# Padding tiles that move the weights against the columns in SBUF: an fp32r attention-plus-GLU kernel

## The chip, the cores and the metric

The kernel runs on one core of a Trainium2 chip. The metric is the device time of one execution in microseconds. Before the change the median of three runs is 695.43 us (695.39 to 695.55). The page of the profile is of one further execution, which took 695.5 us.

The engines are called as the profile calls them: PE (TensorE matmuls), PEld (its weight loads, which overlap the matmuls), DVE (VectorE), ACT (ScalarE), POOL (GpSimd) and SP (SyncE, which here issues most DMAs). SBUF is the on-chip memory that PE reads its two operands from.

## The reference

Two branches work on the same normalised input, and both are added to the input:

```python
xn = layernorm(x)                                   # x: 2048 tokens x 448
return x + A(xn, wq, wk, wv, wo, beta) + B(xn, w_gate, w_up, w_down)

# A: 16 heads of 28, in 4 segments of 512 tokens
q, k, v = xn @ wq, xn @ wk, xn @ wv
for s in range(4):
    p = softmax(q_s @ k_s.T * 28 ** -0.5 + causal_mask)
    num, den = phi(q_s) @ M, phi(q_s) @ z + 1e-6    # phi(t) = t + 1 if t > 0 else exp(t)
    o_s = g * num / den + (1 - g) * (p @ v_s)       # g = sigmoid(beta)
    M, z = M + phi(k_s).T @ v_s, z + sum(phi(k_s))
A = concat(o) @ wo

# B: hidden width 1792
B = (sigmoid(xn @ w_gate) * (xn @ w_up)) @ w_down
```

## The kernel before

The 2048 tokens are cut into 4 blocks of 512, and the 448 features into chunks of 128 partitions. Large products are made in fp32r on PE. Each operand is split into a high part (the value as fp32r rounds it) and a low part (the rest), and three partial products are added in PSUM: high by high, high by low, low by high. For a contraction of 448 this makes 11 matmuls to one PSUM tile (the list `TERMS`).

A matmul has two operands in SBUF: the *weights* (128 columns of one tile, brought into the array by a weight load ahead of it) and the *columns* that are then moved past them. In `T.matmul(out, weights, columns)` they are the second and the third argument. Five groups of fp32r matmuls matter here:

| line | PSUM tile | what | weights | columns | columns moved | matmuls |
|---|---|---|---|---|---|---|
| L241 | `pgu` | gate and up projections | `wgu` | `xs` | 512 | 1232 |
| L347 | `pp` | keys and queries | `wqk` | `xs` | 512 | 308 |
| L166 | `pd` | down projection | `hh` | `wdn` | 448 | 672 |
| L327 | `pv` | values | `xs` | `wv` | 448 | 176 |
| L763 | `po` | output projection | `xs` | `wo` | 448 | 176 |

A sixth one, L604 (`st`, 256 matmuls), makes the attention scores: weights and columns are both slices of one tile `qk2`, on 84 partitions, with 512, 384, 256 or 128 columns.

The order of the work on PE is written out by hand. A front phase (to about 155 us) makes the values, keys and queries. Then the generator `gated()` makes the GLU branch in groups of 11 `pgu` matmuls, with `pd` groups of 6 (in two halves of 3) between them, while `attention()` is stepped between these pieces and puts in the scores (`st`) and the products with the values (`pa`, L679). At the end `project()` makes the output projection, with the last `pd` groups between its first tiles. ACT and DVE split the weights and bring the results out of PSUM, POOL masks the scores, SP issues the loads.

Where a tile lies in SBUF follows from the order in which the pools are opened and from the sizes of their tiles. First comes the pool `keep` (`ident`, `xs`, `acc`, and the small `gate` and `gate_n`), then `mid` (the 8 KB tiles `wgu`, `wo`, the 4 KB tiles `hh`, and staging), then `late` (`wv`, later `wdn`, by the helper `late_pair`), then `front` (`wqk` and more, in the front phase) or `att` (`qk2` and more, later) behind it. All slices that these matmuls take are multiples of 256 bytes away from the start of their tile: 512 columns of fp32 are 2048 bytes, 128 are 512, and 448 are 1792, which is 7 times 256. So the address modulo 256 of an operand is that of its tile, and the difference between the two operands of a line is one number:

| line | columns, address mod 256 | weights, address mod 256 | columns minus weights, mod 256 |
|---|---|---|---|
| L241 `pgu` | `xs` 128 | `wgu` 192 | 192 |
| L347 `pp` | `xs` 128 | `wqk` 192 | 192 |
| L166 `pd` | `wdn` 192 | `hh` 192 | 0 |
| L327 `pv` | `wv` 192 | `xs` 128 | 64 |
| L763 `po` | `wo` 192 | `xs` 128 | 64 |
| L604 `st` | `qk2` 192 | `qk2` 192 | 0 |

In what follows "distance" is the number in the last column.

Of the kernel before, what the change touches and what calls it, by code (L numbers as in the profile page):

```python
# [9 lines left out]
F32 = mybir.dt.float32  # L10
F32R = mybir.dt.float32r
# [5 lines left out]
P = 128  # L17
# [44 lines left out]
def kernel(  # L62
# [13 lines left out]
    keep = ctx.enter_context(tc.tile_pool(name="keep", bufs=1))  # L76
# [7 lines left out]
    def split(hi, lo, src):  # L84
        A.activation(hi, src, AF.Copy)
        V.tensor_sub(lo, src, hi.bitcast(F32))
# [32 lines left out]
    gate = keep.tile([P, NG], F32, name="gate")  # L119
    gate_n = keep.tile([P, NG], F32, name="gate_n")  # L120

    def weigh(pool, num, g, add):

        r = pool.tile([P, 16], F32, name="rc", bufs=2)
        n3 = num.rearrange("p (m c) -> p m c", c=32)
        if add:
            V.tensor_scalar_add(r, n3[:, :, DH], add)
            V.reciprocal(r, r)
        else:
            V.reciprocal(r, n3[:, :, DH])  # L130
        V.scalar_tensor_tensor(n3[:, :, :DH], n3[:, :, :DH], g, r.unsqueeze(2).to_broadcast([P, 16, DH]),
                               op0=ALU.mult, op1=ALU.mult)
# [8 lines left out]
    def eight_k(dtype, name):  # L141
        return mid.tile([P, 8, 256], dtype, name=name, tag="8k")
# [7 lines left out]


    late = ctx.enter_context(tc.tile_pool(name="late", bufs=4, reuse_waits="tile"))

    def late_pair(name):
        return late.tile([P, 2, D], F32R, name=name, tag="late")

    rest, begin, wo = [], [], {}

    def gated():
# [33 lines left out]
            split(wdn[f][:, 0, :], wdn[f][:, 1, :], raw_down[f])  # L193

        def ready_out(h):
            wo[h] = eight_k(F32R, "wo").rearrange("p c n -> p (c n)")
            split(wo[h][:, :2 * D], wo[h][:, 2 * D:4 * D], raw_up[NF + h][:, :2 * D])

        begin.extend([lambda: ready_down(0), lambda: (ready_down(1), load_down(2)), lambda: ready_down(2)])
# [10 lines left out]
        for f0 in range(0, NF, FG):  # L210
# [7 lines left out]
            if f0 + FG < NF:  # L218
                ahead[1, 2] = lambda: ready_up(f0 + 2)
                if f0 > 0:  # L220
                    ahead[2, 1] = lambda: ready_down(f0 + 2)
                ahead[2, 3] = lambda: load_down(f0 + 3)
                ahead[2, 2] = lambda: load_up(f0 + 4)
                ahead[3, 2] = lambda: ready_up(f0 + 3)
                ahead[3, 3] = lambda: ready_down(f0 + 3)
                if f0 > 0:
                    ahead[0, 2] = lambda: (load_up(f0 + 3), load_down(f0 + 2))
            else:

                ahead[0, 2] = lambda: load_up(f0 + 3)  # L230
                ahead[1, 2] = lambda: ready_out(0)
                ahead[3, 2] = lambda: ready_out(1)
# [35 lines left out]

    with tc.tile_pool(name="front", bufs=2) as sb, tc.manual_schedule(engines=FRONT):
        heads = sb.tile([P, P], F32, name="heads", bufs=1)  # L270
        stage = eight_k(F32, "stage").rearrange("p (c a) n -> p c (a n)", c=4)
        vst = eight_k(F32, "vst").rearrange("p (t a) (h c) -> p t (a h) c", t=NT, c=32)
        wv = [late_pair("wv") for _ in range(4)]
# [115 lines left out]
        def recall(b, i, phi):  # L389
            ts = sb.tile([P, L], F32, name="ts", bufs=1)  # L390
            tb = sb.tile([P, L], F32, name="tb", bufs=2)
            n2 = bank("n2", ("m", "pd")[i % 2])
            T.matmul(n2, mst[b % 2][i], phi, start=True, stop=True)  # L393
            V.transpose(ts, n2)
            weigh(sb, ts, gate[:, i:i + 1], MEM_EPS)
            V.transpose(tb, ts)
            nc.gpsimd.dma_start(od[b][P * i:P * (i + 1)], tb)
# [98 lines left out]
        for b in range(NB):  # L496
# [24 lines left out]
            for k, c in enumerate((3, 4, 5, 6, 0, 1, 2) if last else range(7)):  # L521
# [34 lines left out]
                n = k - 1 if b == 0 else k + 1  # L556
# [16 lines left out]
    sb = ctx.enter_context(tc.tile_pool(name="att", bufs=1, reuse_waits="tile"))  # L573
# [88 lines left out]
    class Unit:  # L662
# [10 lines left out]
        def finish(self):  # L673

            s, i = self.s, self.i
            pa = bank("pa", "m")
            for kb in range(NT):
                for j in range(HG):
                    T.matmul(pa[32 * j:32 * j + 32, kb * P:], self.vv[:, kb, 32 * j:32 * j + 32],  # L679
                             self.pairs[j // 2].block(j % 2, kb), start=kb == 0, stop=kb == NT - 1)  # L680
            on, oc = (self.pairs[1].w[:, n * L:(n + 1) * L] for n in range(2))
            V.transpose(on, pa)
            yield
            weigh(sb, on, gate_n[:, i:i + 1], 0.0)
            V.transpose(oc, on)
            nc.gpsimd.dma_start(od[s][P * i:P * (i + 1)], oc, accum_op=ALU.add if s > 0 else ALU.bypass)
            yield
# [138 lines left out]
```

## Time and profile before

| what | value |
|---|---|
| median of the runs | 695.43 us |
| the profiled execution | 695.5 us |
| its span, first to last instruction | 693.8 us |
| PE busy | 688.1 us of the span |
| DVE busy | 570.4 us |
| ACT busy | 344.0 us |
| POOL busy | 147.7 us |
| granted TensorE clock | 1.00 |

The profile gives a matmul a start and a length. Matmuls are pipelined, so the length of one reaches over the start of the next one. What a matmul costs in a stream is therefore the time from its start to the start of the next; it is called its *step* here, and is read from two rows of the timeline: the difference of their starts, divided by the matmuls in the first row. The timeline merges equal instructions that follow each other, and gives the start of the first.

### The profile page before, as it was taken

The numbers are of one execution on the slowest core, as the hardware profiler recorded it, in microseconds if no ns is written. First come the engines' busy times: TensorE is split into PE (matmuls) and PEld (weight loads), VectorE is DVE, ScalarE is ACT, GpSimd is POOL, SyncE is SP. The second block draws the span as 40 slices with busy tenths as digits, with TensorE's granted clock in tenths as the row PEclk, the third lists the DMA queues.
The fourth block names the chain that finished last, engine by engine and source line by source line (L and its number), as shares of the span: only waits on it lengthen the run. The fifth ranks groups of instructions, "written<-read, shape, count | busy, mean of one in ns | idle before, by whom it ended". The sixth has DMA issues, their size and how long they took to land.

```text
span 693.8 us, 10446 instructions
## 1 busy us (share of the span) xinstructions
PE 688.1 (99%) x3594; PEld 565.7 (82%) x3594; DVE 570.4 (82%) x994; ACT 344.0 (50%) x563; POOL 147.7 (21%) x349
## 2 busy tenths in 40 slices
PE   8999999999999999999999999999999999999997
PEld 7898878778878787787878878787787878878897
DVE  6765785767889898988898889998889889889863
ACT  5836555343555456544555446455543555446320
POOL 3400020101223122221222223222232322222000
PEclk9999999999999999999999999999999999999999
DMA  7446566696242323233233342324342332333342
GB/s 265 180 147 236 196 220 228 255 326 169 70 99 73 92 86 85 69 118 106 56 71 93 74 127 56 98 56 115 81 113 57 95 71 68 86 87 88 96 149 106
DMA packets 45796, 84.37 MB, mean 122 GB/s; under 512 B 6320, under 2 KB 20400, under 8 KB 45232
## 3 DMA queue, kind: packets, MB, share of 16 engines
q1 hardware_dynamic: 42736, 76.37, 35.9%
q0 software_dynamic: 3008, 7.34, 5.2%
q8 instruction: 28, 0.46, 0.3%
q14 instruction: 24, 0.20, 0.1%
HBM read 51.05 MB, written 32.64 MB: 121 GB/s over the span
## 4 chain that ended last, share of the span: by engine, by line
PE 97%; DMA 1%; DVE 1%; SPq 0%; ACT 0%; issue 0%
PE pgu L241 42%; PE pd L166 20%; PE pp L347 10%; PE st L604 6%; PE pa L679 5%; PE po L763 5%; PE pv L327 4%; PE pmm L375 2%; PE n L393 1%; DMA acc<-in_x 1%; PE pt L95 1%; PE pk L367 1%; DVE stats L286 0%; DVE acc L767 0%; DVE xs L102 0%
## 5 line engine op out<-in xcount | busy, mean ns | idle before, releaser
L241 PE MATMUL pgu<-xs,wgu 128*128 128x512 f32 x1232 | 320.9, 398 | 0.0
L241 PEld LDWEIGHTS pgu<-xs,wgu 128*128 128x128 f32 x1232 | 226.3, 188 | 48.3 <-issue 3.2
L166 PE MATMUL pd<-wdn,hh 128*128 128x448 f32 x672 | 162.3, 368 | 0.0
L166 PEld LDWEIGHTS pd<-wdn,hh 128*128 128x128 f32 x672 | 123.1, 188 | 15.3 <-issue 1.0
L619 POOL TENSOR_SCALAR_AFFINE_SELECT w<-w 128x256 f32<-128x256 f32 (+1 forms) x160 | 81.0, 507 | 255.0 <-ACT w L608 215.0
L659 ACT ACTIVATE w<-w 128x1024 f32<-128x1024 f32 (+1 forms) x96 | 87.1, 915 | 87.5 <-DVE w L658 85.7
L658 DVE TENSOR_TENSOR w<-w,mb 128x1024 f32<-128x1024 f32 (+1 forms) x96 | 99.6, 1048 | 0.2
L608 ACT ACTIVATE w<-st 128x512 f32<-128x512 f32 x128 | 75.0, 588 | 43.4 <-PE st L604 43.3
L621 DVE TRANSPOSE_TENSOR_REDUCE mx<-w 128x32 f32<-128x1024 f32 x64 | 79.0, 1235 | 12.7 <-POOL w L619 12.7
L347 PE MATMUL pp<-xs,wqk 128*128 128x512 f32 x308 | 79.0, 405 | 0.0
L169 DVE TENSOR_TENSOR acc<-pd,acc 128x448 f32<-128x448 f32 x112 | 67.4, 601 | 2.7 <-PE pd L166 2.5
L347 PEld LDWEIGHTS pp<-xs,wqk 128*128 128x128 f32 x308 | 56.8, 188 | 14.5 <-issue 2.4
L604 PE MATMUL st<-qk 84*128 84x128 f32 (+3 forms) x256 | 64.0, 311 | 0.0
L252 ACT ACTIVATE hh<-sg 128x512 fp32r<-128x512 f32 x56 | 35.1, 626 | 43.9 <-DVE sg L250 34.8
L604 PEld LDWEIGHTS st<-qk 84*128 84x128 f32 x256 | 48.3, 189 | 8.9 <-ACT w L608 0.4
L249 ACT ACTIVATE sg<-pgu 128x512 f32<-128x512 f32 x56 | 33.3, 595 | 39.9 <-PE pgu L241 39.9
L648 DVE STREAM_TRANSPOSE mb<-top 128x1024 f32<-128x1024 f32 x32 | 39.8, 1242 | 10.3 <-POOL top L645 10.1
L354 DVE TENSOR_TENSOR qk<-pp,qk 128x512 fp32r<-128x512 f32 x28 | 19.3, 688 | 31.0 <-ACT e L352 24.9
L250 DVE SCALAR_TENSOR_TENSOR sg<-sg,pgu 128x512 f32<-128x512 f32 x56 | 37.4, 667 | 4.7 <-PE pgu L241 4.7
L253 DVE SCALAR_TENSOR_TENSOR hh<-sg,hh 128x512 fp32r<-128x512 f32 x56 | 38.6, 690 | 2.4 <-ACT hh L252 2.2
L327 PE MATMUL pv<-wv,xs 128*128 128x448 f32 x176 | 39.6, 376 | 0.4 <-DVE xs L102 0.3
L679 PE MATMUL pa<-w,vv 128*32 128x128 f32 (+3 forms) x512 | 38.5, 436 | 0.0
(100 smaller groups left out, 638.8 us busy)
## 6 DMA issues: line engine op xcount, KB each, us to landing
qk<-qd SPq DMA_DIRECT2D x192, 112.0 KB
qd<-qk SPq DMA_DIRECT2D x28, 512.0 KB
raw<-in_w_ffn SPq DMA_DIRECT2D x14, 512.0 KB
vd<-vst SPq DMA_DIRECT2D x4, 1024.0 KB
vv<-vd SPq DMA_DIRECT2D x16, 256.0 KB
od<-w POOLq DMA_DIRECT2D x16, 256.0 KB, 4.0
sums<-od SPq DMA_DIRECT2D x32, 128.0 KB
out<-acc SPq DMA_DIRECT2D x16, 224.0 KB
```

What stands on the lines that cost most here:

```text
L166: T.matmul(pd[:, :D], l, r, start=n == 0, stop=n == len(mms) - 1)
L169: V.tensor_add(acc[b][:, t, :], pd[:, :D], acc[b][:, t, :])
L241: T.matmul(dst, wgu[f][:, w, side * P:(side + 1) * P], xs[b][:, a, :], start=n == 0, stop=n == len(TERMS) - 1)
L327: T.matmul(pv[:, :D], xs[b][:, a, t * P:(t + 1) * P], wv[w], start=n == 0, stop=n == len(TERMS) - 1)
L347: T.matmul(pp, wqk[c][:, w, :], xs[b][:, a, :], start=n == 0, stop=n == len(TERMS) - 1)
L604: T.matmul(st[:, at:at + L - kb * P], self.qk[:KS, 1, h, kb * P:(kb + 1) * P], self.qk[:KS, 0, h, kb * P:], start=True, stop=True)
L608: A.activation(w, st, AF.Copy)
L619: G.affine_select(d, d, pattern=pattern, base=0, channel_multiplier=-1, compare_op=ALU.is_ge, fill=MASK)
L621: V.tensor_reduce(mx[:, 16 * (n - 1):16 * (n + 1)], w3[:, n // 2, :2 * L].rearrange("p (b n) -> p b n", n=32), axis=mybir.AxisListType.X, ...
L658: V.tensor_sub(w, w, m)
L659: A.activation(w, w, AF.Exp, scale=SCALE)
L679: T.matmul(pa[32 * j:32 * j + 32, kb * P:], self.vv[:, kb, 32 * j:32 * j + 32], self.pairs[j // 2].block(j % 2, kb), start=kb == 0, stop=k ...
```

## The change

Tiles that nothing writes or reads are allocated in three pools, and the tiles behind them move. `pad(keep, 192)` stands at the end of `keep`, so everything in `mid` moves by 192 bytes: `wgu`, `hh` and `wo` come from 192 to 128 modulo 256. `pad(late, 64)` stands at the start of `late`: with the 192 from ahead, `wv` and `wdn` move by 256, and so does `qk2` in the pool `att` behind; they stay at 192. `pad(sb, 192)` stands in `front` behind the tile `heads`, so `wqk` comes from 192 to 128. The output projection's weights are now a slice that starts 16 floats (64 bytes) into their tile, so their slices stay at 192.

| line | distance before | distance after |
|---|---|---|
| L241 `pgu`, 512 columns | 192 | 0 |
| L347 `pp`, 512 columns | 192 | 0 |
| L166 `pd`, 448 columns | 0 | 64 |
| L327 `pv`, 448 columns | 64 | 64 |
| L763 `po`, 448 columns | 64 | 64 |
| L604 `st` | 0 | 0 |

In the built program every engine has the same instructions in the same order as before; only addresses differ. Staging tiles, small tiles and operands of DVE, ACT, POOL and the DMAs move with their pools, all by multiples of 64 bytes modulo 256.

```diff
@@ behind gate, gate_n in the pool keep
+    def pad(pool, nbytes):
+        pool.tile([P, nbytes // 4], F32, name="pad", tag="pad", bufs=1)
+
+    pad(keep, 192)
@@ behind the opening of the pool late
+    pad(late, 64)
@@ ready_out
-            wo[h] = eight_k(F32R, "wo").rearrange("p c n -> p (c n)")
+            wo[h] = eight_k(F32R, "wo").rearrange("p c n -> p (c n)")[:, 16:]
@@ the pool front
         heads = sb.tile([P, P], F32, name="heads", bufs=1)
+        pad(sb, 192)
```

## The prediction

> **What bounds the kernel now.** First the page's busy times and its chain of what ended last.
>
> ```profile
> PE 688.1 (99%) x3594; PEld 565.7 (82%) x3594; DVE 570.4 (82%) x994; ACT 344.0 (50%) x563; POOL 147.7 (21%) x349
> ```
> ```profile
> PE 97%; DMA 1%; DVE 1%; SPq 0%; ACT 0%; issue 0%
> PE pgu L241 42%; PE pd L166 20%; PE pp L347 10%; PE st L604 6%; PE pa L679 5%; PE po L763 5%; PE pv L327 4%; PE pmm L375 2%; PE n L393 1%; DMA acc<-in_x 1%; PE pt L95 1%; PE pk L367 1%; DVE stats L286 0%; DVE acc L767 0%; DVE xs L102 0%
> ```
>
> PE is the bound from end to end, and the lines whose distance changes (L241, L347, L166) hold 72% of the chain. The question is only how long one matmul takes. The groups by form give a mean length for each shape:
>
> ```profile
> L241 PE MATMUL pgu<-xs,wgu 128*128 128x512 f32 x1232 | 320.9, 398 | 0.0
> L166 PE MATMUL pd<-wdn,hh 128*128 128x448 f32 x672 | 162.3, 368 | 0.0
> L347 PE MATMUL pp<-xs,wqk 128*128 128x512 f32 x308 | 79.0, 405 | 0.0
> ...
> L763 PE MATMUL po<-wo,xs 128*128 128x448 f32 x176 | 36.5, 363 | 0.0
> L604 PE MATMUL st<-qk 84*128 84x512 f32 x64 | 25.6, 399 | 0.0
> L604 PE MATMUL st<-qk 84*128 84x384 f32 x64 | 21.7, 340 | 0.0
> ...
> L604 PE MATMUL st<-qk 84*128 84x128 f32 x64 | 14.2, 222 | 0.0
> ```
>
> Two lines move 448 columns and differ in nothing but tiles and distance: `pd` at distance 0 has 368 ns, `po` at 64 has 363. Means hold the few matmuls that waited, so the medians of the views by line come next.
>
> ```profile
> L241 PE MATMUL pgu<-xs,wgu x1232: 388/394/795, 133.2 to 643.5; 128*128 128x512 f32 x176
> ...
> L347 PE MATMUL pp<-xs,wqk x308: 390/394/797, 19.8 to 151.0; 128*128 128x512 f32 x154
> ...
> L166 PE MATMUL pd<-wdn,hh x672: 358/365/472, 167.9 to 667.8; 128*128 128x448 f32 x168
> ...
> L763 PE MATMUL po<-wo,xs x176: 360/363/472, 645.0 to 689.9; 128*128 128x448 f32 x176
> ```
>
> Minimum, median and maximum stand in the middle: `pd` 365, `po` 363; both lines of 512 columns, which share distance 192, have 394.
>
> A length reaches over the next start, so the steps are read from the timeline of PE. In the GLU phase:
>
> ```profile
> 296.02 2.72 PE L241 MATMUL pgu<-xs,wgu 128*128 128x512 f32 x11
> 298.58 0.40 PE L604 MATMUL st<-qk 84*128 84x512 f32 x1
> 298.82 0.37 PE L166 MATMUL pd<-wdn,hh 128*128 128x448 f32 x1
> ...
> 519.65 2.49 PE L241 MATMUL pgu<-xs,wgu 128*128 128x512 f32 x10
> 521.99 0.40 PE L604 MATMUL st<-qk 84*128 84x512 f32 x1
> 522.22 1.38 PE L166 MATMUL pd<-wdn,hh 128*128 128x448 f32 x6
> 523.45 2.03 PE L241 MATMUL pgu<-xs,wgu 128*128 128x512 f32 x8
> 525.31 0.40 PE L604 MATMUL st<-qk 84*128 84x384 f32 x2
> ...
> 526.31 1.37 PE L166 MATMUL pd<-wdn,hh 128*128 128x448 f32 x6
> 527.52 0.40 PE L604 MATMUL st<-qk 84*128 84x256 f32 x2
> ```
>
> `pgu` at 192: (2.56 + 2.34 + 1.86) us over 11 + 10 + 8 matmuls is 233.1 ns a step. `pd` at 0: (1.23 + 1.21) us over 12 is 203.3 ns. Single `st` matmuls of 512 columns at 0: 0.24 and 0.23 us, about 235 ns. And in the last phase, where `pd` and `po` stand side by side:
>
> ```profile
> 653.09 1.40 PE L166 MATMUL pd<-wdn,hh 128*128 128x448 f32 x6
> 654.33 2.37 PE L763 MATMUL po<-wo,xs 128*128 128x448 f32 x11
> 656.54 1.37 PE L166 MATMUL pd<-wdn,hh 128*128 128x448 f32 x6
> 657.75 2.36 PE L763 MATMUL po<-wo,xs 128*128 128x448 f32 x11
> 659.95 1.40 PE L166 MATMUL pd<-wdn,hh 128*128 128x448 f32 x6
> 661.19 2.37 PE L763 MATMUL po<-wo,xs 128*128 128x448 f32 x11
> 663.40 1.37 PE L166 MATMUL pd<-wdn,hh 128*128 128x448 f32 x6
> 664.61 2.36 PE L763 MATMUL po<-wo,xs 128*128 128x448 f32 x11
> 666.81 1.40 PE L166 MATMUL pd<-wdn,hh 128*128 128x448 f32 x6
> 668.05 22.17 PE L763 MATMUL po<-wo,xs 128*128 128x448 f32 x110
> ...
> 689.66 0.56 PE L763 MATMUL po<-wo,xs 128*128 128x448 f32 x2
> ```
>
> The five `pd` groups take 1.24 + 1.21 + 1.24 + 1.21 + 1.24 = 6.14 us, 204.7 ns a step. `po` at 64 takes 200.1 ns in its unbroken run (21.61 us over 108).
>
> **The change part by part.** *The pads.* No instruction is added, so they cost no time of their own. What moves with them on DVE, ACT, POOL and in the DMAs I cost at nothing. The cover is their idle time while PE runs the GLU phase:
>
> ```profile
> 170.00:640.00 470.00, 470.00 (x2493) 381.10 (x2492) 418.48 (x676) 243.64 (x381) 119.28 (x298) 1.00 0.34 84
> ```
>
> Here, in the order PE, PEld, DVE, ACT, POOL, PE is busy all 470.00 us and DVE, the next engine, 418.48. If PE gets faster by 1%, DVE still has over 40 us to spare, and what would come late first without that cover are the PSUM tiles of L604, which ACT empties. No queue is passed by anything, no wait is added.
>
> *The `wo` slice.* It keeps `po` at 64, and `pv` stays there too: 0 for both.
>
> *`pd`, 448 columns, from 0 to 64.* The price is in the trace: the step of the same shape at 64. From 203.3 to 200.1 ns are 3.2 ns, times 672 is 2.1 us, all on the path. Ends: 2 ns by the medians (1.3 us), 4.6 ns by the last phase (3.1 us). I take 2.1, from the phase where most `pd` stand.
>
> *`pgu` and `pp`, 512 columns, from 192 to 0.* 1540 matmuls, so one nanosecond of step is 1.54 us, and no row shows these lines at 0. I bound the step. From above: `st` of 512 columns at 0. Its mean length of 399 ns lies 5 above the median of 394 at distance 192; a length exceeds the step by about 162 ns (394 - 233, 365 - 203, 363 - 200), which makes 237, and its starts say 235: I take 236, or 2.9 ns worse than now. But `st` uses 84 partitions and stands alone between other groups, which never lets it settle. From the `pd` row: 203.3 ns at 0, plus 64 more columns. In the rows of `st` 128 columns cost 59 ns (340 - 222 is 118 for 256, 399 - 340 is 59), so 64 cost 29.5, and the step is 232.8, or 0.3 better. From below: if 0 is for 512 columns what 64 is for 448, 200.1 + 29.5 = 229.6, or 3.5 better. The last two use full groups on 128 partitions, as `pgu` does, so they are nearer than `st`; I take their middle, 231.2: 1.9 ns, times 1540 is 2.9 us.
>
> *Sum.* 695.5 us for the profiled execution (span 693.8 and 1.7 around it), 0.07 above the median, so the sum is made against 695.43: less 2.1, less 2.9, is **690.4 us**.
>
> [...]
>
> **The rivals.**
>
> *1. Slower: 0 is a bad distance for 512 columns too.* The place is L241 and L347, the price what the `st` rows show, 2.9 ns on 1540 steps, 4.5 us, against the 2.1 that `pd` gains: 697.8. It decides from 1.4 ns on (2.1 us / 1540). For it: 0 is the worse distance in both pairs that can be compared (`pd` against `po`, `st` against `pgu`). Against it: the `st` rows are single matmuls in another group's wake.
>
> *2. Nothing happens.* The difference of `pd` and `po` would be one of their surroundings (groups of 6 against long runs), not of distance: 695.4. For it: the weight loads have the same length at all distances:
>
> ```profile
> L241 PEld LDWEIGHTS pgu<-xs,wgu 128*128 128x128 f32 x1232 | 226.3, 188 | 48.3 <-issue 3.2
> L166 PEld LDWEIGHTS pd<-wdn,hh 128*128 128x128 f32 x672 | 123.1, 188 | 15.3 <-issue 1.0
> ```
>
> Against it: in the last phase `po` keeps about 200.6 ns in groups of 11 between `pd` groups (2.21, 2.20, 2.21, 2.20 us), so broken runs alone do not make 204.7. [...]
>
> *3. A whole notch.* The steps that repeat stand on a lattice: 200.1, 206.7 (1.24 us over 6 `pd`) and 233.1 are about 30, 31 and 35 times 6.67 ns. If a distance decides on which notch a long run locks, `pgu` and `pp` may drop one, 6.67 ns on 1540 steps, 10.3 us, with `pd` 683.0. For it: `po` is one notch under the slower `pd` groups. Against it: runs broken every 3 to 11 matmuls lie between notches, as `pd` does at 203.3.
>
> **How the numbers follow.** Runs of this kernel agree within 0.16 us, but I call all within 0.2% (1.4 us) the same. My forecast has 0.40, with a range of its own from 688 to 693 (512 columns at 229.6 to 232.8, `pd` by its ends); rival 1 has 0.24, with less than its full price in a few of these; rival 2 0.14; rival 3 0.22. Faster: forecast and rival 3, and a little of the rest, 0.64. Slower: most of rival 1, 0.20. Same: rival 2 and the remainder, 0.16. The range goes from rival 3's 683 to rival 1's 698.
>
> **What would show it.** After the change the median length of L166 should be 363, as that of L763, with steps near 200; a median of 365 refutes the first term. The medians of L241 and L347 should be about 392: 394 means rival 2 for that term, 397 rival 1, 387 rival 3. L763 and L327 should stay at 363, `st` at its lengths. I am wrong if the two lines of 512 columns part, if idle time of PE appears at L604, or if lengths change where the distance did not.

## The result, and the profile after

The changed kernel takes 691.38 us (median of 6 runs, 691.24 to 692.0) against 695.47 us before (6 runs, 695.39 to 695.56). The ratio is 0.9943, with a 95% interval from 0.993 to 0.9956: 4.1 us faster, where 5.0 were forecast. The profiled execution has a span of 689.6 us, 693.8 before.

The page of the changed kernel, busy times and the chain of what ended last (lines are 7 or 8 higher than before: `pgu` is L248, `pd` L173, `pp` L355, `po` L771, `st` L612, `pa` L687):

```profile
PE 682.4 (99%) x3594; PEld 565.6 (82%) x3594; DVE 569.7 (83%) x994; ACT 342.6 (50%) x563; POOL 146.0 (21%) x349
...
PE 77%; DVE 10%; issue 7%; POOL 3%; ACT 1%; DMA 1%; SPq 0%; POOLq 0%; ACTq 0%
```

PE is still busy 99% of the span, but the chain is no longer PE alone: 97% have become 77%, and DVE, POOL and ACT hold 14%. These shares are not time lost: where PE waited, however briefly, the chain goes on along the engine that it waited for. The lengths by line (minimum, median, maximum in ns), each row the first of the view of its line:

```profile
L248 PE MATMUL pgu<-xs,wgu x1232: 387/390/796, 132.0 to 639.5; 128*128 128x512 f32 x176
...
L355 PE MATMUL pp<-xs,wqk x308: 387/389/801, 19.7 to 149.5; 128*128 128x512 f32 x154
...
L173 PE MATMUL pd<-wdn,hh x672: 360/363/473, 166.0 to 663.6; 128*128 128x448 f32 x168
...
L771 PE MATMUL po<-wo,xs x176: 360/362/476, 640.9 to 685.6; 128*128 128x448 f32 x176
```

The two lines of 512 columns went from 394 to 390 and 389, `pd` from 365 to 363. The steps stand in the timeline of PE, at the places that the prediction read:

```profile
293.51 2.68 PE L248 MATMUL pgu<-xs,wgu 128*128 128x512 f32 x11
296.03 0.40 PE L612 MATMUL st<-qk 84*128 84x512 f32 x1
296.26 1.38 PE L173 MATMUL pd<-wdn,hh 128*128 128x448 f32 x6
297.48 0.40 PE L612 MATMUL st<-qk 84*128 84x384 f32 x2
...
518.33 1.38 PE L173 MATMUL pd<-wdn,hh 128*128 128x448 f32 x6
519.54 1.97 PE L248 MATMUL pgu<-xs,wgu 128*128 128x512 f32 x8
521.35 0.40 PE L612 MATMUL st<-qk 84*128 84x384 f32 x2
...
652.42 1.36 PE L173 MATMUL pd<-wdn,hh 128*128 128x448 f32 x6
653.62 2.36 PE L771 MATMUL po<-wo,xs 128*128 128x448 f32 x11
```

`pgu` takes 2.52 us over 11 and 1.81 us over 8, 229 and 226 ns a step, where it took 233. `pd` takes 1.22 and 1.21 us over 6, 202 to 203 ns, hardly less than before; only in the last phase, between `po` groups, is it at 1.20 us over 6, 200 ns, where it was at 204.7.

Adding up the time from each matmul's start to the next start, line by line over the whole trace, gives the balance (`pa` is the product of the attention weights with the values):

| line | before, us | after, us | difference |
|---|---|---|---|
| `pgu` | 292.4 | 288.5 | -3.9 |
| `pp` | 75.0 | 73.7 | -1.3 |
| `pd` | 138.8 | 138.6 | -0.2 |
| `pa` | 37.3 | 38.5 | +1.2 |
| all others | 144.8 | 144.8 | 0.0 |
| all | 688.3 | 684.1 | -4.2 |

So the 512-column lines gave 5.2 us, `pd` almost nothing, and `pa`, whose distance did not change, took 1.2 us back. The mean step, without the steps over 245 ns (where a group starts or PE waits), went from 233.2 to 229.7 ns for `pgu`, from 233.1 to 228.8 for `pp` and from 202.8 to 202.0 for `pd`.

### The profile page after: what moved, and what is told of

Its sections match the earlier page's. It is cut to its first block, busy times and chain, and to the rows that moved or that the text cites. A ratio compares the mean times of both kernels' runs of the same rounds, so it can differ in the third digit from the quotient of the medians.

```text
span 689.6 us, 10445 instructions
## 1 busy us (share of the span) xinstructions
PE 682.4 (99%) x3594; PEld 565.6 (82%) x3594; DVE 569.7 (83%) x994; ACT 342.6 (50%) x563; POOL 146.0 (21%) x349
## 4 chain that ended last, share of the span: by engine, by line
PE 77%; DVE 10%; issue 7%; POOL 3%; ACT 1%; DMA 1%; SPq 0%; POOLq 0%; ACTq 0%
PE pgu L248 30%; PE pd L173 14%; PE pp L355 10%; PE po L771 5%; PE pv L335 5%; PE st L612 4%; PE pa L687 4%; DVE mx L629 2%; POOL w L627 2%; PE pmm L383 2%; PE n L401 1%; DVE acc L176 1%; DVE w L666 1%; DMA acc<-in_x 1%; PE pt L95 1%
## 5 line engine op out<-in xcount | busy, mean ns | idle before, releaser
L248 PE MATMUL pgu<-xs,wgu 128*128 128x512 f32 x1232 | 316.8, 395 | 0.0
L248 PEld LDWEIGHTS pgu<-xs,wgu 128*128 128x128 f32 x1232 | 226.6, 188 | 45.0 <-issue 3.2
L173 PE MATMUL pd<-wdn,hh 128*128 128x448 f32 x672 | 161.8, 367 | 0.0
L173 PEld LDWEIGHTS pd<-wdn,hh 128*128 128x128 f32 x672 | 123.0, 188 | 14.5 <-issue 0.6
L627 POOL TENSOR_SCALAR_AFFINE_SELECT w<-w 128x256 f32<-128x256 f32 (+1 forms) x160 | 79.1, 496 | 251.5 <-ACT w L616 216.3
L355 PE MATMUL pp<-xs,wqk 128*128 128x512 f32 x308 | 77.7, 401 | 0.0
L355 PEld LDWEIGHTS pp<-xs,wqk 128*128 128x128 f32 x308 | 56.8, 188 | 13.4 <-issue 2.4
L612 PE MATMUL st<-qk 84*128 84x128 f32 (+3 forms) x256 | 64.1, 311 | 0.4 <-ACT w L616 0.3
L259 ACT ACTIVATE hh<-sg 128x512 fp32r<-128x512 f32 x56 | 35.1, 626 | 47.3 <-DVE sg L257 37.3
L612 PEld LDWEIGHTS st<-qk 84*128 84x128 f32 x256 | 48.4, 189 | 9.3 <-ACT w L616 1.9
L257 DVE SCALAR_TENSOR_TENSOR sg<-sg,pgu 128x512 f32<-128x512 f32 x56 | 37.4, 668 | 4.3 <-PE pgu L248 4.3
L687 PE MATMUL pa<-w,vv 128*32 128x128 f32 (+3 forms) x512 | 39.6, 436 | 0.1
```

Of the source, the lines that this page charges most:

```text
L173: T.matmul(pd[:, :D], l, r, start=n == 0, stop=n == len(mms) - 1)
L248: T.matmul(dst, wgu[f][:, w, side * P:(side + 1) * P], xs[b][:, a, :], start=n == 0, stop=n == len(TERMS) - 1)
L355: T.matmul(pp, wqk[c][:, w, :], xs[b][:, a, :], start=n == 0, stop=n == len(TERMS) - 1)
L612: T.matmul(st[:, at:at + L - kb * P], self.qk[:KS, 1, h, kb * P:(kb + 1) * P], self.qk[:KS, 0, h, kb * P:], start=True, stop=True)
L627: G.affine_select(d, d, pattern=pattern, base=0, channel_multiplier=-1, compare_op=ALU.is_ge, fill=MASK)
```

## The experiments

The theory to be tested: the step of a matmul is set, line by line, by the distance of its columns from its weights modulo 256 bytes. The rivals: the addresses themselves count; the surroundings of a group count and not its distance; the gain sits in `pd`.

**The 512-column lines alone.** In the pool `mid` a pad of 64 bytes goes between the 8 KB and the 4 KB tiles, and `late` has none, so `wgu` and `wqk` stand at distance 0 while `pd` stays at 0.

```diff
+        pad(mid, 64)
         raw = [four_k(F32, "wv_raw") for _ in range(2)]
...
-    pad(late, 64)
```

> Only the 512-column lines get distance 0 (gate/up and key/query); the down projection keeps distance 0, values and output projection keep 64. Theory (the step of a matmul is set by the distance between its columns and its weights, line by line): the trace of the changed kernel has 3.5 ns less per gate/up step and 4.3 per key/query step, 5.3 us together, and 0.5 us less on the down projection, so about 691.9 us here, 0.5 above the changed kernel. As the prediction split it (2.9 and 2.1 us): 692.6 us. Rival (the down projection's distance carries the gain, the 512-column lines only settle differently behind it): 694 us or more.

Measured: 691.69 us (691.52 to 692.09), ratio 0.9946 [0.9933, 0.9958]. All but 0.3 us of the gain is there, and 0.3 us is inside the spread. The rival of the expectation, 694 us or more, fell.

**The down projection alone.** On the kernel before, the 4 KB tiles `hh` move by 192 bytes and the pool `late` by 256; `wgu` and `wqk` stay at distance 192 modulo 256.

```diff
+        pad(mid, 192)
         raw = [four_k(F32, "wv_raw") for _ in range(2)]
...
+    pad(late, 64)
```

> Only the down projection gets distance 64; the 512-column lines keep 192. As predicted (3.2 ns on 672 steps): 693.4 us, median length 363 ns. By the trace of the changed kernel (0.8 ns a step): 695.0 us. Rival (its gain depends on what the 512-column group ahead leaves behind): anything from 693.4 to 695.5, and the two single changes do not add up to the gain of both.

Measured: 695.56 us (695.39 to 695.75), ratio 0.9999 [0.999, 1.0008]. Distance 64 alone gives nothing for `pd`, not the 0.5 us of the expectation either. The view of its line:

```profile
L171 PE MATMUL pd<-wdn,hh x672: 360/365/477, 168.0 to 667.9; 128*128 128x448 f32 x168
```

The median is 365, as before, at distance 64. In the sums of steps `pd` lost 0.14 us and `pgu`, which the run does not touch, took 0.22 more. The two single gains, 3.9 and 0.0 us, add up to the 4.1 us of both within the spread.

The same run moves `wqk` and `wv` by 256 bytes against `xs`: the sum of the `pp` steps stays at 75.0 us and the median of `pv` steps at 201 ns. So far as this one move shows it, 256 bytes more make no difference.

**Everything moved, no distance changed.**

```diff
     ident = keep.tile([P, P], F32, name="ident")
     make_identity(nc, ident)
+    keep.tile([P, 16], F32, name="pad")
     xs = [keep.tile([P, 7, L], F32R, name=f"xs{b}") for b in range(NB)]
```

> Kernel before, with all tiles from the activations on moved by 64 bytes together: every distance is as before, every address is another. Theory (distance alone counts): 695.5 us, medians 394 ns for 512 columns and 365 for the down projection, as before. Rival (the address of weights or columns itself counts, by its place modulo 256): several us off, since the weights of the 512-column lines then stand at 0 modulo 256 and the columns at 192.

Measured: 695.63 us, ratio 1.0001 [0.9992, 1.001]. Its lines:

```profile
L242 PE MATMUL pgu<-xs,wgu x1232: 388/394/795, 133.3 to 643.7; 128*128 128x512 f32 x176
...
L167 PE MATMUL pd<-wdn,hh x672: 358/365/472, 168.1 to 668.0; 128*128 128x448 f32 x168
```

The medians and the minima are those of before. A shift of 64 bytes that leaves the distances as they are changes nothing, and changing the distance of the 512-column lines alone gave 3.9 us. So it is the distance that counts, not the addresses themselves, at this one shift.

**Unbroken streams.** Behind the end of the kernel before, slices of `xs` are multiplied with slices of `xs` at any distance:

```diff
+    def stream(name, cols, far, count):
...
+            T.matmul(out[:, :cols], left[:, 512 + at:512 + at + P], right[:, 512 + at + far // 4:][:, :cols],
+                     start=True, stop=True)
+        for cols in (512, 448):
+            for far in range(0, 256, 32):
+                stream(f"alone{cols}at{far}x", cols, far, 48)
```

> Kernel before, and behind its end unbroken streams of 48 matmuls with 512 and with 448 columns at distances 0, 32, 64, ... 224, then groups of 11 with 512 columns and of 6 with 448 in turn at the four pairs of distances (192 and 0, 192 and 64, 0 and 0, 0 and 64); their results are not used. Theory (distance sets the step): 448 columns 200.1 ns at 64 and 203 to 207 at 0, 512 columns 233.1 at 192 and 226.7 to 230 at 0; in the turns the 448-column steps at 64 lose a part of their lead over 0. Rival (surroundings, not distance): all streams of one width have one step. Whole time about 695.5 + 16 x 48 x 0.215 + 24 x (11 x 0.231 + 6 x 0.203), about 951 us.

The timeline of these streams, 48 matmuls in each row; a step is the difference to the next row's start over 48:

```profile
690.03 11.04 PE L794 MATMUL alone512at0x<-xs,xs 128*128 128x512 f32 x48
700.91 11.37 PE L794 MATMUL alone512at32x<-xs,xs 128*128 128x512 f32 x48
712.11 11.16 PE L794 MATMUL alone512at64x<-xs,xs 128*128 128x512 f32 x48
723.11 11.37 PE L794 MATMUL alone512at96x<-xs,xs 128*128 128x512 f32 x48
...
756.76 11.35 PE L794 MATMUL alone512at192x<-xs,xs 128*128 128x512 f32 x48
767.95 11.35 PE L794 MATMUL alone512at224x<-xs,xs 128*128 128x512 f32 x48
779.14 9.90 PE L794 MATMUL alone448at0x<-xs,xs 128*128 128x448 f32 x48
788.88 10.07 PE L794 MATMUL alone448at32x<-xs,xs 128*128 128x448 f32 x48
798.79 9.76 PE L794 MATMUL alone448at64x<-xs,xs 128*128 128x448 f32 x48
808.39 10.01 PE L794 MATMUL alone448at96x<-xs,xs 128*128 128x448 f32 x48
```

512 columns: 10.88 us over 48 at distance 0, 226.7 ns; 233.3 at 32; 229.2 at 64; 233.1 at 192 (11.19 us over 48). 448 columns: 202.9 at 0, 206.5 at 32, 200.0 at 64. The distances not quoted here have 233.3 (128) and 234.2 (160) for 512 columns; for 448 columns 128 has 204.0, 160 has 200.0, 192 has 202.2 and 224 has 204.2. So the step of these streams goes with the distance: for 512 columns 0 is the best of these eight, for 448 columns 64 and 160. In the turns of 11 and 6 the lead of 64 over 0 for 448 columns, 2.9 ns in a stream, shrinks to 1.2 ns behind 512 columns at 192 (202.4 and 201.2) and to 0.7 behind 512 at 0 (202.1 and 201.4). The starts show where a short group falls behind a stream: a group of 11 with 512 columns at 0, behind 6 with 448 at 0, steps 236, 229, 232, 231 ns and only then 226 to 227 to its end.

**The 512-column lines at 64.** The changed kernel, `keep` padded by 128 and the 4 KB tiles by 64 more.

```diff
-    pad(keep, 192)
+    pad(keep, 128)
...
-            wo[h] = eight_k(F32R, "wo").rearrange("p c n -> p (c n)")[:, 16:]
+            wo[h] = eight_k(F32R, "wo").rearrange("p c n -> p (c n)")[:, 32:]
...
+        pad(mid, 64)
         raw = [four_k(F32, "wv_raw") for _ in range(2)]
...
-        pad(sb, 192)
+        pad(sb, 128)
```

> Changed kernel, but the 512-column lines at distance 64 in place of 0; the 448-column lines at 64 as there. Theory (the streams' steps carry over): 64 has 228.9 ns in a stream, 0 has 226.7, 192 has 233.3, so two thirds of the gain of 0: about 692.7 us, medians near 391. Rival (any distance but 192 gives the kernel the same gain): 691.4.

Measured: 692.62 us (692.32 to 692.87), ratio 0.9956 [0.9942, 0.9969]. That is the 692.7 worked out from the streams. Its medians were expected near 391 and came to 392 for `pp` and 394 for `pgu`, the value of before:

```profile
L248 PE MATMUL pgu<-xs,wgu x1232: 387/394/801, 132.6 to 640.9; 128*128 128x512 f32 x176
```

The mean step of `pgu` fell all the same, from 233.2 to 230.9 ns, so the median of the lengths is a poor sign here. The order of the streams carries over to the kernel, and 64 has about two thirds of the gain of 0 in both (2.9 of 4.1 us here, 4.0 of 6.5 ns a step in the streams). Of the streams' size only about half arrives: at distance 0 the 5.2 us of `pgu` and `pp` are 3.4 ns on each of 1540 steps, where the stream has 6.5.

**The down projection at 160.**

```diff
-    pad(late, 64)
+    pad(late, 160)
...
-        pad(sb, 192)
+        pad(sb, 96)
```

> Changed kernel, with down projection and values at distance 160 in place of 64; 512 columns stay at 0. Theory (groups of 3 and 6 never settle, and 64 needs a few matmuls to reach its 200 ns, while the stream at 160 had 200 from its second matmul on): down projection 202.0 to about 200.2 ns a step, 1.2 us less, 690.2 us. Rival (the down projection's distance does nothing in this kernel): 691.4 us.

Measured: 692.77 us (692.73 to 692.87), 1.4 us slower than the changed kernel. The theory of this run fell, and so did its rival. Its lines `pd` and `pv`, which also went from 64 to 160:

```profile
L173 PE MATMUL pd<-wdn,hh x672: 358/366/477, 166.5 to 665.1; 128*128 128x448 f32 x168
...
L335 PE MATMUL pv<-wv,xs x176: 360/367/772, 8.8 to 125.6; 128*128 128x448 f32 x176
```

`pv` rose from 363 to 367, though it runs in groups of 11 to 44. By the starts in the trace `pv` steps went from 200.3 to 203.3 ns, `pd` from 202.0 to 203.6, and `pgu`, whose distance was not touched, from 229.7 to 230.7. In sums that is 0.5, 0.8 and 1.2 us more, and `pa` has 0.7 less: the largest part of the loss, 1.2 us, stands at a line that was not changed. The 203.3 of `pv` is a mean of two rhythms (patterns of steps that repeat), as two runs of it in the timeline show, each with the row behind it:

```profile
44.30 9.33 PE L335 MATMUL pv<-wv,xs 128*128 128x448 f32 x44
53.47 5.19 PE L355 MATMUL pp<-xs,wqk 128*128 128x512 f32 x22
...
78.04 4.66 PE L335 MATMUL pv<-wv,xs 128*128 128x448 f32 x22
82.54 1.02 PE L401 MATMUL n<-phi,mst 112*128 112x512 f32 x2
```

Without the first step, which is 290 and 288 ns, the run of 44 takes 206.5 ns a step, the run of 22 takes 200.6. So at 160 two runs of 448 columns had two rhythms, 206.5 and 200.6 ns. What decides which one a run takes is not shown.

**Streams with narrower weights, finer distances, and the kernel's own groups.**

```diff
+        for wide in (128, 96, 64, 32):
+            for cols, far in ((512, 192), (512, 0), (448, 32), (448, 64)):
+                stream(f"wide{wide}for{cols}at{far}x", cols, far, 36, wide)
...
+        for b in range(0, 256, 32):
+            for _ in range(4):
+                stream(f"eight0with{b}x", 512, 0, 8)
+                stream(f"three{b}x", 448, b, 3)
+                stream(f"three0with{b}x", 512, 0, 3)
+                stream(f"six{b}x", 448, b, 6)
```

> Kernel before, with streams behind its end, results not used. (1) Streams with 128, 96, 64 and 32 weight columns. Theory (the loss comes from reading the weights while columns are read): with fewer weight columns the steps at 192 (512 columns) and 32 (448 columns) fall towards those at 0 and 64, and all fall towards a common floor. Rival (the columns' reading has its own loss, the weights only set its phase): 512 columns stay above 226 ns whatever the weights. (2) Distances 16, 48, 80 and so on: if the effect goes by 32 or 64 bytes, they equal a neighbour of the first streams; if it is finer, they have values of their own. (3) Weights that stand in turn at two distances: if the distance of a matmul to its own weights counts, steps of 226.7 and 233.3 alternate; if that to the next weights counts, they alternate shifted by one. (4) Groups of 8 and 3 with 512 columns at 0, and between them 3 and 6 with 448 columns at each distance, as the kernel has them: 160 should have the shortest 448-column steps, since its stream stood at 200 ns from the first matmul on, about 200 against 201 to 202 at 64 and 0.

The timeline of the streams with 128 and with 32 weight columns, 36 matmuls in each row:

```profile
689.89 8.56 PE L794 MATMUL wide128for512at192x<-xs,xs 128*128 128x512 f32 x36
698.29 8.34 PE L794 MATMUL wide128for512at0x<-xs,xs 128*128 128x512 f32 x36
706.47 7.60 PE L794 MATMUL wide128for448at32x<-xs,xs 128*128 128x448 f32 x36
713.91 7.37 PE L794 MATMUL wide128for448at64x<-xs,xs 128*128 128x448 f32 x36
...
783.68 8.48 PE L794 MATMUL wide32for512at192x<-xs,xs 128*32 128x512 f32 x36
792.00 8.49 PE L794 MATMUL wide32for512at0x<-xs,xs 128*32 128x512 f32 x36
800.33 7.48 PE L794 MATMUL wide32for448at32x<-xs,xs 128*32 128x448 f32 x36
807.65 7.58 PE L794 MATMUL wide32for448at64x<-xs,xs 128*32 128x448 f32 x36
```

With 128 weight columns the distances 192 and 0 differ by 6 ns (8.40 and 8.18 us over 36: 233.3 and 227.2). With 32 they are the same, 231.1 and 231.4. For 448 columns the order turns over, 203.3 ns at 32 (7.32 us over 36) and 206.1 at 64, where 128 weight columns have 206.7 and 200.1. Between them the order is mixed: 96 weight columns have 228.3 at 192 and 230.0 at 0, 64 have 232.5 and 229.9. So the number of weight columns matters: with fewer of them the ranking of the distances is another. But the step does not fall to a common floor; with 32 it is above the 227 that 128 weight columns have at 0, so the theory of part 1 falls, and its rival, a step above 226 ns whatever the weights, stands. Where the loss arises is not shown by that: with fewer weight columns fewer partitions are written, too (`out[:wide]` in the kernel of this run), and no run takes the two apart.

Finer distances have values of their own (512 columns: 231.6 at 16, 233.3 at 48, 235.7 at 240, none below 231), so the effect does not go by whole 32 or 64 bytes. Weights in turn at two distances gave 229.9 ns (0 and 192 in turn, 231.7 two by two) and 203.3 ns (32 and 64 away in turn), the two single turns with a pattern of four or six matmuls rather than two; whether the own weights or the next ones count can't be told from that and stays open.

In the groups as the kernel has them (8, 3, 3, 6), each distance has four turns, and its time is the difference of its first row to the first row of the next distance:

```profile
972.79 2.02 PE L794 MATMUL eight0with0x<-xs,xs 128*128 128x512 f32 x8
...
990.17 1.98 PE L794 MATMUL eight0with32x<-xs,xs 128*128 128x512 f32 x8
...
1007.63 2.00 PE L794 MATMUL eight0with64x<-xs,xs 128*128 128x512 f32 x8
...
1025.08 2.02 PE L794 MATMUL eight0with96x<-xs,xs 128*128 128x512 f32 x8
```

80 matmuls take 17.38 us with 448 columns at 0 and 17.45 us with 64. At 64 the 448-column steps are shorter (201.6 and 200.3 ns in the groups of 3 and 6, against 203.1 and 202.8 at 0), but the 512-column steps between and behind them, at distance 0 in both, are longer (234.2 and 231.5 against 231.7 and 228.0). The 448 columns at 96 have 205.7 and 205.8, and the 512-column steps beside them 226.9 and 229.8. What one group gains the next gives back here: the 512-column groups, at 0 throughout, change by up to 7 ns with their neighbours' distance. Their first steps go with the group ahead: behind 6 at 0 the 8 step 226 and 227 ns from the start (turns 2 to 4), behind 6 at 64 they step about 236, 233, 236, 224, 231. 160 has 205.2 and 204.5 ns here, which agrees with the run above and refutes part 4 of the expectation.

**The pace of the attention.** To see where the 1.2 us of `pa` went, the attention is stepped a little thinner through the GLU phase.

```diff
-LEAD, TAIL = 15, 53
+LEAD, TAIL = 13, 53
```

> Changed kernel, with the attention stepped from 2 places earlier on (LEAD 13 in place of 15), so its work is spread a little thinner over the GLU phase. Theory (the steps of the three lines are 5.5 us shorter in the trace, and 1.2 us of that is given back in waits of scores and of products with the values for ACT and DVE, which the faster PE now reaches first): some of the 1.2 us returns, 690.4 to 691.2 us, with fewer waits at the scores. Rival (the give-back has another place, or the pace only moves it): 691.4 us or more.

Measured: 690.95 us (690.86 to 690.98), ratio 0.9934 [0.9921, 0.9946], 0.4 us below the changed kernel. The other end, `TAIL` 50 in place of 53:

> Changed kernel, with the attention ending 3 places later (TAIL 50 in place of 53), thinner over the GLU phase from the other end. Theory as for the earlier start: 690.4 to 691.2 us, unless the output projection at the end now waits for the last attention; rival: 691.4 us or more.

Measured: 691.06 us (690.8 to 691.85), ratio 0.9938 [0.9924, 0.9952]; the spread reaches into that of the changed kernel. And both together:

> Changed kernel with both looser paces (LEAD 13, TAIL 50). Theory (each alone returned 0.3 to 0.4 us of what the waits had given back, 1.2 us in all): 690.5 to 690.9 us. Rival (what can return has returned): 690.95 or more.

Measured: 690.77 us (690.75 to 691.23), ratio 0.9934 [0.9921, 0.9948]. The waits of the weight loads of `pa` and `st`: the kernel before first, then the changed kernel, then the one with `LEAD` 13:

```profile
PEld pa L679 <- ACT w L659: 0.8, 2, 0.6
PEld st L604 <- ACT w L608: 0.4, 1, 0.4
```
```profile
PEld st L612 <- ACT w L616: 1.9, 4, 0.7
PEld pa L687 <- POOL w L627: 1.7, 5, 0.4
...
PEld pa L687 <- ACT w L667: 1.4, 2, 0.8
```
```profile
PEld st L612 <- ACT w L616: 2.6, 5, 0.8
...
PEld pa L687 <- POOL w L627: 1.4, 4, 0.4
...
PEld pa L687 <- ACT w L667: 0.4, 2, 0.3
```

In these lists (total us, times, longest) `pa` waits 1.4 us for ACT's exponentials in the changed kernel, 0.8 before, and `st` waits 1.9 us for ACT to empty a bank, 0.4 before. Four of the 16 groups of `pa` hold the 1.2 us: those that start at 289.2 us (32 matmuls in 3.03 us, 2.29 before) and 436.8 us (3.21, 2.97 before) have 1.0 of it, and the two waits for the exponentials. The first of them in the changed kernel's timeline of weight loads:

```profile
290.78 1.22 PEld L687 LDWEIGHTS pa<-w,vv 128*32 128x32 f32 x20 [0.61 <-ACT w L667]
```

With `LEAD` 13 the wait of `pa` for ACT falls to 0.4 us, and the sum of the `pa` steps is 37.4 us, against 37.3 before the change. But the waits of `st` grew to 2.6 us, where the expectation had fewer, and by the runs only 0.4 us came back, 0.6 with both paces. So the place of the give-back is shown, and most of it moves when it is chased. 690.77 us is the lowest median of all, with the changed kernel's distances; its 0.2 us below `LEAD` 13 alone lie inside its own spread (690.75 to 691.23).

## Why the prediction was right, and which of its terms were not

The direction, the range and the sum held: 690.4 forecast, 691.38 measured, and the step of the 512-column lines did fall by their distance, as the forecast's mechanism has it. Two terms were off, in opposite directions, and a third was missing. That the sum came within 1 us is in part luck: against the steps in the trace `pd` was 1.9 us too high, `pgu` and `pp` 2.3 us too low, and the wait of 1.2 us had no term. The forecast's own range is also narrower than its ends: they add up to 686.9 and 693.6, not 688 and 693; the measured time lies in both.

*`pd`, 2.1 us, was mis-sized: 0.0 measured alone (695.56 against 695.55), 0.2 in the steps of the changed kernel.* The step that failed is "the price is in the trace: the step of the same shape at 64". 200.1 ns was the step of `po` in a run of 110; `pd` runs in groups of 3 and 6 between 512-column groups and `st`, and the prediction used that very fact against rival 3 without applying it to its own first term. In its groups `pd` went from 202.8 to 202.0 ns. The fall that the last phase promised, from 204.7, did come, to 200.0, but only in the few groups that stand between `po`. The median of its lengths came to 363, as the prediction asked, with steps of 202: the sign was given, and the term was not there.

*`pgu` and `pp`, 2.9 us, were mis-sized the other way: 3.9 us alone as measured, 5.2 us in the steps.* The middle of 229.6 and 232.8 ns was taken; the steps came to 229.7 (`pgu`) and 228.8 (`pp`), at the lower end. What misled is the `pd` row as a measure of distance 0: in the streams 0 is a middling distance for 448 columns (202.9 ns, where the eight lie between 200.0 and 206.5) and the best one for 512 (226.7). The ranking does not carry from one of these widths to the other.

*Nothing was put down for a wait that takes over.* The cover that was named, DVE's idle share of the GLU phase, is an average; at `pa` and `st` the exponentials and the emptied banks come late (waits of 1.4 and 1.9 us in the changed kernel, 0.8 and 0.4 before), and `pa` alone took 1.2 us. The prediction named idle time of PE at `st` as a sign against it, and it appeared, once, with 0.3 us.

*The rivals.* Rival 1 fell: the single `st` matmuls at 0, 235 ns, stand in the wake of other groups and say nothing of a run, which is at 226.7 in the streams. Rival 2 fell for the 512-column lines (all distances kept, nothing changed; one distance changed, 3.9 us) and held in effect for `pd`. The equal lengths of the weight loads, put down for it, did not tell: those of `pgu` have 188 ns before and after, while its step went from 233.2 to 229.7. Through what the distance acts no run here shows. Rival 3 was right for unbroken runs, 233.3 to 226.7 is its one notch, and its own counter-argument was right for the kernel, where `pgu`, at 229.7, is about half a notch above 226.7.

## What to carry to other kernels

Where one engine's stream of matmuls is the whole time, place their two operands on purpose: on this chip, for fp32r, a distance modulo 256 bytes between columns and weights was worth 3% of a step at 512 columns in an unbroken stream (226.7 ns at 0, 233.1 at 192) and about half of that in this kernel's groups (229.7 and 233.2), and unused tiles of 64 and 192 bytes set it. Measure the distances for each width in the groups that the kernel really runs: here `pgu` in its groups stayed at 229.7 ns where the stream has 226.7, and groups of 8 at one distance began with steps of 226 or 236 ns, by the group ahead. After a gain on the bounding engine look at which wait comes up behind it (here `st` for ACT, from 0.4 to 1.9 us), and loosen the pace there.

## What the runs showed of the hardware

The steps of several unbroken streams lie on a lattice whose spacing, fitted to them, is 6.67 ns: 200.0 (448 columns at 64 and 160), 206.7 (448 at 32, in the streams of 36), 226.7 (512 at 0) and 233.3 ns (512 at 32 and 128) are 30, 31, 34 and 35 of these. Two streams cycle between two notches, and their cycle is near a whole number of them: the stream of 448 columns at 192 repeats 199, 201, 207 ns, together 607 or 91 of them, and the stream of 512 at 64 repeats 226, 229, 232, together 687 or 103.

In the trace before, 807 of the 1232 `pgu` starts, taken modulo 20/3 ns, lie in one fifth of that period, where an even spread would put 246, though waits stand between them; in the changed kernel 530 of 1232 do. A run repeats patterns such as 231, 236, 231, 236 or 233, 233, 234 (both in the trace before, 512 columns at 192), and the first steps of a group change with the group ahead of it, as the groups of 8 above show. What makes this period was not found, and why the step goes with the distance is open too.
